# Convolution stem, forward and backward: one leaf product shared by the even and odd halves of the last five chunks of the input gradient

## The chip, the cores and the metric

The kernel runs on one core of a Trainium2 chip. Times are device microseconds of one execution. The kernel before takes 1117.52 us, the median of three runs (1116.88, 1117.52, 1117.68). One more execution was recorded by the profiler; its rows are what the profile shows.

A core has a matrix engine (TensorE, PE in the profile, its weight loads PEld), which writes its sums to PSUM; VectorE (DVE) and ScalarE (ACT) for element-wise work; GpSimd (POOL) and SyncE (SP), which here mostly issue transfers. Each engine takes its instructions in the order in which they were written into its queue.

## The reference

A strided convolution over time, a normalisation over time for each channel, and a GELU; and the gradients of all that.

```python
def _fwd_reference(x, w, gn_gamma, gn_beta):          # x (2, 16000, 256), w (31, 256, 256)
    s = 2
    L = (T - K) // s + 1                              # 7985
    h = jnp.einsum('blc,cd->bld', x[:, 0:s * L:s, :], w[0])
    for i in range(1, K):
        h = h + jnp.einsum('blc,cd->bld', x[:, i:i + s * L:s, :], w[i])
    mu = jnp.einsum('bld->bd', h)[:, None, :] / L
    var = jnp.einsum('bld->bd', (h - mu) ** 2)[:, None, :] / L
    h = (h - mu) / jnp.sqrt(var + 1e-5)
    h = h * gn_gamma[None, None, :] + gn_beta[None, None, :]
    return _gelu(h)
...
    _out, _vjp = jax.vjp(_f, x, w, gn_gamma, gn_beta)
    _grads = _vjp(grad_out)
    _out0 = jnp.asarray(_out)
    return (_out0, *[jnp.asarray(_g) for _g in _grads])
```

Everything is bf16. `out_1` is the gradient of `x`: each of its rows is a sum over taps of the gradient of the convolution's output times a transposed weight.

## The kernel before

**Products.** The 31 taps are split by three binary digits. Two of them are treated as in Karatsuba's multiplication of polynomials: instead of four products of halves there are three (of the first halves, of the last halves, and of sums or differences). Done twice, this gives three branches A, B, C (the order of work is B, A, C, `ORDER`), and in each of them three leaf products, again A, B and C. Sums and differences of inputs and of weights are made on DVE beforehand; the leaf products are corrected and added up afterwards.

**Stages.** F0 and F1 are the forward pass of the two batches (matmul line L505), G0 and G1 the gradient of the input (`input_grad`, matmul line L1131), W the gradient of the weight (matmul line L1346). The gradient of the input goes over two batches `b`, four chunks `c` of 256 positions (one position is 16 rows of `out_1`), two halves `pr` of 128 positions in each, and the three branches. With t = 4b + c, the chunks t = 3 to 7 are the last five; in them all three branches take the shorter way with a shared outer product (the set `GOC`), which before only branch B does.

**One branch of one half, in the last five chunks.** Two PSUM pairs, `px` and `pt`, each hold two banks of 512 columns. The stationary operand of a matmul is 128 positions of the (summed) gradient, the moving one 512 columns of weights.
- `g_outer(pt, ..., C_)`: 4 matmuls; ACT copies the result into `px` (`g_copy`, L1160).
- `g_three_b`: the middle leaf's first part, 4 matmuls on top of that copy; ACT copies bank 0 of `px` to bank 1 (L1160).
- `g_outer(pt, ..., A)`: 4 matmuls; `g_delta` copies the result to SBUF (L1160, out to the arena).
- `g_three_ac(px, br, B_, ...)`: the middle leaf's second part, two groups of 4 matmuls, one for each bank.
- `g_seed`: DVE writes `pt` as `px` less the saved copy (L1194), as the start for leaf A.
- `last(A)` and `last(C_)`, called while the next branch is under way: two groups of 4 matmuls each, then `g_evac`.

`g_evac` moves finished banks out of PSUM: for branch B to `GSB`, for A and C by ACT (`keep`, L584) into the output tile `HO`, to which DVE adds `GSB` (L1208). Each half has an output tile of its own (`HO[pr]`); after branch C's last leaf one transfer of 1 MB writes the 128 positions to `out_1`, issued by SP (the helper `load`, L313). Sums for the next chunk are made by DVE in `g_sums` (L1077) and `e_comp` (L1028), in the same stretch of time. Leaf operands for W are turned by DMA (L318) and stored to DRAM (`dl_turn`).

**Order.** A planner (`Plan`) records each operation, 3333 in all, with what it reads and writes; the order in which they are emitted, and so the order within each engine's queue, is a table of operation numbers in the kernel's text (`SEQUENCE`). Nothing is scheduled at run time: an instruction waits for its inputs by semaphores, and what stands behind it on its engine waits with it.

**Seam to W.** W begins with `leaf_d` (L1512: four subtractions of 2304 elements, into the tiles `DL`), `pair_x` (L1412, L1416) and `pair_d` (L1427, L1432), all on DVE; `DL` lies at byte 146880 of the arena, and `HO[1]` at 144128 reaches over it. SP's queue is shared by the stores of `out_1`, the loads of `x` and the turns.

Of the kernel before, what the change touches and what calls it, by code (L numbers as in the profile page):

```python
# [234 lines left out]
def conv_stem_kernel(  # L235
# [123 lines left out]
    DNO = {True: [sb(GREG + 28928 + 2048 * i, 2, 2, D) for i in range(4)], False: [sb(GREG + o, 2, 2, D) for o in (0, 2048, 25088, 27136)]}  # L359
    assert GREG + 37952 <= REG  # L360

    DG, DGT = sb(209664, P), sb(209920, P)
    ident = DGT


# [767 lines left out]

    def g_wide(br, lf, q):
        return 512 if i_tap(3 - q, 1, MIR[br], MIR[lf]) < K else 256

    def g_leaf(ps, br, lf, pl, o, fresh):
        w2 = W2[MIR[br]]
        for e in range(2):
# [546 lines left out]
```

## Time and profile before

| | us |
|---|---|
| median of three runs | 1117.52 |
| profiled execution, its own time | 1116.78 |
| its span, from the first to the last instruction | 1115.0 |
| PE busy in the span | 1089.1 |
| DVE busy | 920.6 |
| ACT busy | 577.9 |
| PE at L505 (forward), busy | 396.3 |
| PE at L1131 (gradient of the input), busy | 390.3 |
| PE at L1346 (gradient of the weight), busy | 302.8 |

Matmuls overlap, so the busy time of PE is the time in which at least one of them is under way, and the mean duration of one is longer than the distance between two starts. A group of instructions in the profile is named by line, engine, operation and operands (out, then in); behind a bar stand its busy time, the mean duration in ns, and the idle time just before its instructions with what ended most of it. L1131 and L505 and the like are lines of the kernel before. The chain of waits goes back from the last instruction to what released each one.

### The profile page before, as it was taken

To read this page: it belongs to the slowest core of one execution; us is meant where nothing else is said; L and a number is where in the kernel's file an instruction comes from. 1 tells how busy PE (TensorE), PEld (TensorE's weight loads), DVE (VectorE), ACT (ScalarE), POOL (GpSimd) and SP (SyncE) were. 2 spreads that over 40 slices of the span, in tenths; PEclk is the share of its full clock that TensorE was granted. 3 is DMA by queue.
4 is the path that set the end of the run, shared out by engine and by line. 5 is a ranking of instruction groups with operands and counts; after the bars stand their busy time and mean duration, and the time that the engine had idled before them with its cause. 6 is when DMAs were issued, how large, how long until landed. Compare 5 with 4: busy or idle time off the path is not lost.

```text
span 1115.0 us, 18978 instructions
## 1 busy us (share of the span) xinstructions
PE 1089.1 (98%) x7672; PEld 749.7 (67%) x7672; DVE 920.6 (83%) x894; ACT 577.9 (52%) x880; POOL 130.1 (12%) x233
## 2 busy tenths in 40 slices
PE   6999999999999989999999999999999999999997
PEld 4888899978787974444444444444586777678884
DVE  6986877889999999989897565554799699799995
ACT  1234434588988679899964666554413322202221
POOL 0000000000000003232342423231200000000000
PEclk9999999999999999999999999999999999999999
DMA  9969889867979789999899787778985867998778
GB/s 236 189 181 241 249 222 256 223 149 173 224 168 207 252 317 273 266 248 263 215 236 238 173 195 180 177 209 183 279 277 165 257 201 240 287 269 288 229 209 195
DMA packets 343398, 251.96 MB, mean 226 GB/s; under 512 B 234039, under 2 KB 311485, under 8 KB 338109
## 3 DMA queue, kind: packets, MB, share of 16 engines
q1 hardware_dynamic: 336205, 231.86, 80.5%
q0 software_dynamic: 7104, 18.89, 6.2%
q8 instruction: 60, 0.98, 0.3%
q14 instruction: 29, 0.24, 0.1%
HBM read 112.53 MB, written 82.35 MB: 175 GB/s over the span
## 4 chain that ended last, share of the span: by engine, by line
PE 84%; DVE 7%; SPq 2%; DMA 2%; issue 2%; ACT 1%; POOL 1%; DVEq 0%; POOLq 0%
PE ps L505 32%; PE ps L1131 30%; PE ps L1346 22%; SPq L313 1%; DVE arena L447 1%; DVE arena L463 1%; SPq L318 1%; DVE arena L580 1%; DVE arena L1311 1%; DMA out_dram<-arena 1%; DMA arena<-hd 1%; DVE ps L1456 1%; DMA arena<-in_w_dram 1%; DMA arena<-arena 0%; DVE arena L1416 0%
## 5 line engine op out<-in xcount | busy, mean ns | idle before, releaser
L505 PE MATMUL ps<-arena 128*128 128x256 bf16 (+4 forms) x3464 | 396.3, 278 | 10.5 <-DMA arena<-in_x_dram 6.0
L1131 PE MATMUL ps<-arena 128*128 128x512 bf16 (+1 forms) x1824 | 390.3, 376 | 4.3 <-ACT ps L1160 4.0
L505 PEld LDWEIGHTS <-arena 128*128 128x128 bf16 x3464 | 338.0, 98 | 68.5 <-DMA arena<-in_x_dram 6.2
L1131 PEld LDWEIGHTS <-arena 128*128 128x128 bf16 x1824 | 178.6, 98 | 215.6 <-issue 3.6
L1346 PE MATMUL ps<-arena 128*128 128x256 bf16 (+1 forms) x2384 | 302.8, 290 | 5.3 <-DVE arena L580 1.9
L1346 PEld LDWEIGHTS <-arena 128*128 128x128 bf16 x2384 | 233.1, 98 | 75.1 <-issue 6.4
L584 ACT ACTIVATE arena<-ps 128x1024 bf16<-128x1024 f32 (+1 forms) x121 | 122.3, 1022 | 233.0 <-PE ps L1346 79.1
L463 DVE TENSOR_TENSOR arena<-arena 128x2064 bf16<-128x2064 bf16 (+8 forms) x131 | 163.3, 1264 | 28.6 <-PE ps L505 27.7
L313 POOL DMA_DIRECT2D dld<-arena x144 | 105.6, 735 | 239.0 <-DMA arena<-arena 195.1
L1194 DVE TENSOR_TENSOR ps<-ps,arena 128x1024 f32<-128x1024 f32 x36 | 44.3, 1231 | 69.3 <-PE ps L1131 65.4
L1077 DVE TENSOR_TENSOR arena<-arena 128x1032 bf16<-128x1032 bf16 (+1 forms) x114 | 89.3, 813 | 2.7 <-PE ps L1131 1.7
L550 ACT ACTIVATE ps<-ps 128x256 f32<-128x256 f32 x89 | 36.6, 412 | 87.9 <-PE ps L505 81.8
L1311 DVE TENSOR_TENSOR arena<-arena 128x4096 bf16<-128x4096 bf16 x32 | 72.3, 2283 | 1.9 <-DMA arena<-in_x_dram 1.8
L1160 ACT COPY ps<-ps 128x512 f32<-128x512 f32 x84 | 48.2, 575 | 34.0 <-PE ps L1131 32.6
L322 POOL MEMSET arena<- 128x104 bf16 (+11 forms) x52 | 12.3, 253 | 414.9 <-DVE arena L880 138.1
L918 DVE TENSOR_TENSOR arena<-arena 128x2048 bf16<-128x2048 bf16 (+1 forms) x48 | 57.4, 1197 | 3.0 <-ACT arena L921 1.3
L604 ACT ACTIVATE arena<-ps 128x512 bf16<-128x512 f32 (+1 forms) x64 | 37.0, 585 | 32.4 <-PE ps L505 31.4
L1432 DVE TENSOR_TENSOR arena<-arena 128x2048 bf16<-128x2048 bf16 x40 | 47.8, 1216 | 3.1 <-DMA arena<-dld 1.7
L880 DVE TENSOR_TENSOR arena<-arena 128x2048 bf16<-128x2048 bf16 (+1 forms) x40 | 47.6, 1197 | 2.0 <-ACT arena L872 0.9
L1456 DVE TENSOR_TENSOR ps<-ps,arena 128x1024 f32<-128x1024 f32 x24 | 29.0, 1224 | 16.7 <-PE ps L1346 12.6
L1448 ACT COPY ps<-ps 128x256 f32<-128x256 f32 x54 | 19.1, 360 | 43.0 <-PE ps L1346 42.0
L1517 DVE TENSOR_TENSOR arena<-arena 128x4608 bf16<-128x4608 bf16 x16 | 40.5, 2549 | 0.0
(91 smaller groups left out, 746.9 us busy)
## 6 DMA issues: line engine op xcount, KB each, us to landing
arena<-in_x_dram SPq DMA_DIRECT2D x36, 1024.0 KB
arena<-hd SPq DMA_DIRECT2D x40, 512.0 KB
dld<-arena POOLq DMA_DIRECT2D x144, 128.0 KB, 4.3
out_dram<-arena SPq DMA_DIRECT2D x14, 1024.0 KB
arena<-dld SPq DMA_DIRECT2D x18, 640.0 KB
arena<-dld SPq DMA_DIRECT2D x18, 576.0 KB
vl<-arena SPq DMA_DIRECT2D x36, 256.0 KB
arena<-vl SPq DMA_DIRECT2D x9, 1024.0 KB
```

The costliest lines, as they stand in the source:

```text
L313: lambda: e.dma_start(out=out, in_=in_), dma=np_ * ns / 16e3 * 1.03, ns=ns, tp=SH[pk], slack=slack)
L463: lambda: nc.vector.tensor_tensor(out=o, in0=a, in1=b, op=ALU.add))
L505: yield nc.tensor.matmul(ps[:, dh, cs], lhsT=wt, rhs=mv, start=s0, stop=False, skip_group_check=True)
L584: lambda: nc.scalar.activation(out=out, in_=ps, func=ACT.Copy, scale=scale))
L880: add("DVE", dve(nf), [o], [a, b_], lambda: V.tensor_tensor(out=o, in0=a, in1=b_, op=op))
L918: add("DVE", dve(nf), [o], [a, b_], lambda: V.tensor_tensor(out=o, in0=a, in1=b_, op=op))
L1077: lambda: nc.vector.tensor_tensor(out=o, in0=a, in1=b, op=ALU.subtract))
L1131: yield nc.tensor.matmul(ps[:, e, 0:wide], lhsT=lt, rhs=mv, start=s0, stop=False, skip_group_check=True)
L1160: add("ACT", act(512), [o], [i], lambda: nc.scalar.copy(out=o, in_=i))
L1311: add("DVE", dve(4096), [o], [a, b], lambda: nc.vector.tensor_tensor(out=o, in0=a, in1=b, op=ALU.add))
L1346: yield nc.tensor.matmul(ps[:, s, c0:c1], lhsT=lt, rhs=mv, start=s0, stop=False, skip_group_check=True)
L1432: add("DVE", dve(2048), [o], [u, v], lambda o=o, u=u, v=v: nc.vector.tensor_tensor(out=o, in0=u, in1=v, op=ALU.subtract))
```

## The change

Only for t = 4b + c of 3 and more:

1. The two halves of a chunk are no longer its first and last 128 positions, but its even and its odd ones. The stationary operand is read with a step of two elements (`win`).
2. In branch B the middle leaf is made in another way. Both halves need one product in common, since an odd position's neighbour is an even one: `x_common` makes it once a chunk (4 matmuls, with the weight sum `WS`) and `keep`s it in SBUF (`HX`). For each half `x_own` makes 4 matmuls and a DVE operation that writes both banks of `px` as bank 1 plus `HX`; `x_rest` then adds two groups of 2 matmuls with the difference `DX` of neighbouring positions (`x_diff`, DVE) as stationary operand. `g_three_b` with its ACT copy and `g_three_ac` fall away there.
3. There is one output tile `HO` instead of two; `WS` and `HX` lie in the space of the second, `DX` behind the other tiles.
4. Each half's store is split in two: the rows of branch A after A's last leaf, the rows of branch C after C's, 0.5 MB each in runs of 1024 bytes, to every second block of 16 rows.
5. One more sum on DVE makes `WS`, once, and the table `SEQUENCE` is another over the whole program, with 3369 operations.

```diff
-    HO = [sb(119232, 2, 4, 512), sb(GREG + 16704, 2, 4, 512)]
+    HO = sb(119232, 2, 4, 512)
...
+    XB = B_
+    WS, HX = sb(GREG + 16704, 2, 2, 512), sb(GREG + 20800, 1024, dt=FP32)
+    DX = sb(209056, 2, 2, P)
...
+    def win(o, k):
+        s0, st_ = o
+        return slice(s0 + k, s0 + k + st_ * (P - 1) + 1, st_)
+
+    def x_diff(u, par):
+
+        def at(k):
+            return u.rearrange("p e d f -> p (e d) f")[:, :, k:k + 2 * P - 1:2]
+        o = DX.rearrange("p e d f -> p (e d) f")
+        add("DVE", dve(o.free_size(), 1), [o], [u], lambda: nc.vector.tensor_tensor(out=o, in0=at(2 * par), in1=at(1), op=ALU.subtract))
+
+    def x_common(px, u):
+        for e in range(2):
+            jobs = [(e, 512, u[:, e, dh, win((1, 2), 0)], WS[:, dh, 1 - e], dh == 0) for dh in range(2)]
+            g_mm(px, jobs, [px[:, e]], [WS, u[:, e]])
+        keep(HX, flat2(px))
+
+    def x_own(px, br, pl, o):
+        wd = W2D[MIR[br], B_]
+        g_mm(px, [(1, 512, pl[1][:, dh, win(o, q2)], wd[:, dh, 1 - q2], False) for q2 in range(2) for dh in range(2)],
+             [px[:, 1]], [wd, pl[1], px[:, 1]])
+        v = px[:, 1]
+        v = bass.AP(tensor=v.tensor, offset=v.offset, ap=[list(v.ap[0]), [0, 2], [1, 512]])
+        h = HX.rearrange("p (e f) -> p e f", e=2)
+        add("DVE", dve(1024, 1), [px[:]], [px[:, 1], HX], lambda: nc.vector.tensor_tensor(out=px[:], in0=v, in1=h, op=ALU.add))
+
+    def x_rest(px, br, par):
+        w2 = W2[MIR[br]][:, B_]
+        for e in range(2):
+            k = 3 - 2 * par - e
+            jobs = [(e, 512, DX[:, e, dh], w2[:, dh, k * 512:k * 512 + 512], False) for dh in range(2)]
+            g_mm(px, jobs, [px[:, e]], [w2, DX[:, e], px[:, e]])
...
-                jobs.append((0, 512, pl[1][:, dh, o + q2:o + q2 + P], wd[:, dh, 1 - q2, :], fresh and q2 + dh == 0))
+                jobs.append((0, 512, pl[1][:, dh, win(o, q2)], wd[:, dh, 1 - q2, :], fresh and q2 + dh == 0))
...
-        if br == C_ and lf == C_:
-            n0 = 512 * c + 256 * pr
...
+        if lf == C_ and 4 * b + c >= 3:
+            m0, r = HM * c + pr, P if c < 3 else 116
+            dst = bass.AP(tensor=out_1.tensor, offset=out_1.offset + (b * T + 16 * m0) * C + 512 * r2,
+                          ap=[[32 * C, r], [1024, 4], [1, 512]])
+            load(dst, ho[0:r].rearrange("p e k f -> p (e k) f")[:, r2:8:2], r * 4096, 1024, "POOL", slack=60.0)
...
-                    o = P * pr
+                    o = (P * pr, 1) if t < 3 else (pr, 2)
...
+                            four = t >= 3 and br == XB
+                            if four:
+                                x_diff(GU[br], pr)
+                                if pr == 0:
+                                    x_common(px, GU[br])
                             g_outer(pt, br, planes(br, C_), o, C_)
-                            g_copy(px[:, 0], pt[:, 0])
-                        g_three_b(px, br, B_, planes(br, B_), o, not both)
+                            g_copy(px[:, int(four)], pt[:, 0])
+                        if both and four:
+                            x_own(px, br, planes(br, B_), o)
+                        else:
+                            g_three_b(px, br, B_, planes(br, B_), o, not both)
...
-                        g_three_ac(px, br, B_, GU[br], o)
+                        if both and four:
+                            x_rest(px, br, pr)
+                        else:
+                            g_three_ac(px, br, B_, GU[br], o)
...
+            w2 = W2[MIR[XB]][:, B_].rearrange("p d (q f) -> p d q f", q=4)
+            w_sum(WS, w2[:, :, 0:2], w2[:, :, 2:4])
```

The same change from `o + q2:o + q2 + P` to `win(o, q2)` stands in `g_leaf`, `g_outer` and `g_three_ac`. In the changed kernel the lines behind this place are some fifty further down: L1077 becomes L1081, L1194 L1230, L1208 L1244, L1311 L1362, L1412 L1463, L1416 L1467, L1427 L1478, L1512 L1563.

**The order, first place.** The last half of the last chunk on DVE before, from the sums of its operands on: L1194 is the seed of leaf A in a branch, L1208 the addition to the output tile, L1077 the sums of operands.

```order
L1077 TENSOR_TENSOR arena<-arena 128x2x2x258
L1208 TENSOR_TENSOR arena<-arena 128x4x512
L1077 TENSOR_TENSOR arena<-arena 128x8x258
L1194 TENSOR_TENSOR ps<-ps,arena 128x1024
L1208 TENSOR_TENSOR arena<-arena 128x4x512
L1077 TENSOR_TENSOR arena<-arena 128x8x258 x2
L1194 TENSOR_TENSOR ps<-ps,arena 128x1024 x3
L1208 TENSOR_TENSOR arena<-arena 128x4x512 x2
```

The same place in the changed kernel: L1150 is `x_diff`, L1165 the DVE operation of `x_own`, L1230 the seed of leaf A, L1244 the addition to the output tile.

```order
L1165 TENSOR_TENSOR ps<-ps,arena 128x1024
L1244 TENSOR_TENSOR arena<-arena 128x4x512
L1230 TENSOR_TENSOR ps<-ps,arena 128x1024
L1150 TENSOR_TENSOR arena<-arena 128x512
L1081 TENSOR_TENSOR arena<-arena 128x2x2x258
L1244 TENSOR_TENSOR arena<-arena 128x4x512
L1081 TENSOR_TENSOR arena<-arena 128x8x258 x2
L1230 TENSOR_TENSOR ps<-ps,arena 128x1024 x2
L1244 TENSOR_TENSOR arena<-arena 128x4x512 x2
L1165 TENSOR_TENSOR ps<-ps,arena 128x1024
L1230 TENSOR_TENSOR ps<-ps,arena 128x1024
```

The operation of `x_own`, for which the matmuls of `x_rest` wait, now stands in the queue behind additions to the output tile, and `x_diff` stands early, behind the seed of the branch before.

**Second place: the seam to W on DVE.** Before, the last addition to the output tile (L1208) comes ahead of half of `pair_d` (L1427), `pair_x` (L1412), the four operations of `leaf_d` (L1512) and two more of `pair_x` (L1416).

```order
L1208 TENSOR_TENSOR arena<-arena 128x4x512
L1427 TENSOR_TENSOR arena<-arena 128x1024 x2
L1208 TENSOR_TENSOR arena<-arena 128x4x512
L1427 TENSOR_TENSOR arena<-arena 128x1024 x2
L1412 TENSOR_TENSOR arena<-arena 128x4096
L1512 TENSOR_TENSOR arena<-arena 128x2304 x4
L1416 TENSOR_TENSOR arena<-arena 128x2048 x2
L1456 TENSOR_TENSOR ps<-ps,arena 128x1024 x2
L1432 TENSOR_TENSOR arena<-arena 128x2048 x2
```

In the changed kernel, with L1478 for L1427, L1563 for L1512, L1244 for L1208, L1463 for L1412, L1467 for L1416, L1483 for L1432 and L1507 for L1456:

```order
L1478 TENSOR_TENSOR arena<-arena 128x1024 x4
L1563 TENSOR_TENSOR arena<-arena 128x2304
L1244 TENSOR_TENSOR arena<-arena 128x4x512 x2
L1563 TENSOR_TENSOR arena<-arena 128x2304 x2
L1463 TENSOR_TENSOR arena<-arena 128x4096
L1467 TENSOR_TENSOR arena<-arena 128x2048 x2
L1563 TENSOR_TENSOR arena<-arena 128x2304
L1483 TENSOR_TENSOR arena<-arena 128x2048
```

All four of L1478 and the first of L1563 have moved ahead of the last two additions, and the last of L1563 behind L1467. `leaf_d` no longer writes where an output tile lay; the first L1483, whose target reaches over `HO`, comes seven operations behind the last addition.

**Third place: the start, on DVE.** Before, in the first chunk of the forward pass: L463 are sums of inputs, L447 differences of weights, L580 leaf results moved out of PSUM.

```order
L447 TENSOR_TENSOR arena<-arena 128x2048 x12
L463 TENSOR_TENSOR arena<-arena 128x16x262
L463 TENSOR_TENSOR arena<-arena 128x8x260
L447 TENSOR_TENSOR arena<-arena 128x2048
L463 TENSOR_TENSOR arena<-arena 128x8x260
L447 TENSOR_TENSOR arena<-arena 128x2048
L463 TENSOR_TENSOR arena<-arena 128x8x258
L463 TENSOR_TENSOR arena<-arena 128x2x4x262 x2
L580 TENSOR_TENSOR arena<-ps,arena 128x1024
L463 TENSOR_TENSOR arena<-arena 128x8x260 x2
L580 TENSOR_TENSOR arena<-ps,arena 128x1024
L447 TENSOR_TENSOR arena<-arena 128x2048 x2
```

The changed kernel there, with L467, L451 and L584 for them; the memset of L1642, which was at L1591 and stood later, now comes in ahead of these rows:

```order
L467 TENSOR_TENSOR arena<-arena 128x8x260 x2
L451 TENSOR_TENSOR arena<-arena 128x2048
L467 TENSOR_TENSOR arena<-arena 128x2x4x262
L467 TENSOR_TENSOR arena<-arena 128x8x258
L451 TENSOR_TENSOR arena<-arena 128x2048
L467 TENSOR_TENSOR arena<-arena 128x2x4x262
L584 TENSOR_TENSOR arena<-ps,arena 128x1024
L467 TENSOR_TENSOR arena<-arena 128x8x260
L584 TENSOR_TENSOR arena<-ps,arena 128x1024
L451 TENSOR_TENSOR arena<-arena 128x2048
L467 TENSOR_TENSOR arena<-arena 128x8x260
L451 TENSOR_TENSOR arena<-arena 128x2048
```

One L467 has moved behind the L451 that follows the second L584.

More of the change, by code (lines that the diff above doesn't have):

```diff
@@ L359, in conv_stem_kernel @@
     DNO = {True: [sb(GREG + 28928 + 2048 * i, 2, 2, D) for i in range(4)], False: [sb(GREG + o, 2, 2, D) for o in (0, 2048, 25088, 27136)]}
+    XB = B_
+    WS, HX = sb(GREG + 16704, 2, 2, 512), sb(GREG + 20800, 1024, dt=FP32)
+    DX = sb(209056, 2, 2, P)
     assert GREG + 37952 <= REG
[L362 removed]
+    DG, DGT = sb(210080, P), sb(210336, P)
     ident = DGT
@@ L1143, in g_leaf @@
                 u = pl[(e + q) % 2]
-                oo = o + (e + q) // 2
                 for dh in range(2):
-                    jobs.append((e, wide, u[:, dh, oo:oo + P],
+                    jobs.append((e, wide, u[:, dh, win(o, (e + q) // 2)],
                                  w2[:, MIR[lf], dh, (3 - q) * 512:(3 - q) * 512 + wide], fresh and q + dh == 0))
@@ L1164, in g_outer @@
         wd = (W2DO if lf == A else W2DC)[MIR[br]]
-        jobs = [(0, 512, pl[1][:, dh, o + q2:o + q2 + P], wd[:, dh, 1 - q2, :], lf == C_ and q2 + dh == 0)
+        jobs = [(0, 512, pl[1][:, dh, win(o, q2)], wd[:, dh, 1 - q2, :], lf == C_ and q2 + dh == 0)
                 for q2 in range(2) for dh in range(2)]
@@ L1176, in g_three_ac @@
                 for dh in range(2):
-                    jobs.append((e, wide, u[:, e, dh, o + q2:o + q2 + P],
+                    jobs.append((e, wide, u[:, e, dh, win(o, q2)],
                                  w2[:, MIR[lf], dh, (3 - q) * 512:(3 - q) * 512 + wide], False))
@@ L1200, in g_evac @@
         both = (b, c, br) in GOC
-        ho = HO[pr if both else 0]
+        ho = HO
         r2 = 0 if br == A else 1
@@ L1212, in g_evac @@
                 lambda: nc.vector.tensor_tensor(out=ho[:, :, k, :], in0=ps[:], in1=g, op=ALU.add))
-        if br == C_ and lf == C_:
-            n0 = 512 * c + 256 * pr
-            r = P if c < 3 or pr == 0 else 104
-            load(out_1[b, 8 * n0:8 * n0 + 16 * r, :].rearrange("(p r) c -> p (r c)", r=16),
-                 ho[0:r].rearrange("p e k f -> p (e k f)"), r * 8192, 4096, "POOL", slack=60.0)
+        if lf == C_ and 4 * b + c >= 3:
[3 more added lines that the diff above has]
+            load(dst, ho[0:r].rearrange("p e k f -> p (e k) f")[:, r2:8:2], r * 4096, 1024, "POOL", slack=60.0)
+        elif br == C_ and lf == C_:
+            m0 = HM * c + P * pr
+            load(out_1[b, 16 * m0:16 * (m0 + P), :].rearrange("(p r) c -> p (r c)", r=16),
+                 ho.rearrange("p e k f -> p (e k f)"), P * 8192, 4096, "POOL", slack=60.0)
     G3 = {(b, br, B_) for b in range(NB) for br in ORDER}
```

205 rows, old and new, of the table SEQUENCE are left out of this document.

## The prediction

> **What bounds the kernel now.** I read the page first: the busy shares, the chain that ended last, the costliest groups.
>
> ```profile
> PE 1089.1 (98%) x7672; PEld 749.7 (67%) x7672; DVE 920.6 (83%) x894; ACT 577.9 (52%) x880; POOL 130.1 (12%) x233
> PE ps L505 32%; PE ps L1131 30%; PE ps L1346 22%; SPq L313 1%; DVE arena L447 1%; DVE arena L463 1%; SPq L318 1%; DVE arena L580 1%; DVE arena L1311 1%; DMA out_dram<-arena 1%; DMA arena<-hd 1%; DVE ps L1456 1%; DMA arena<-in_w_dram 1%; DMA arena<-arena 0%; DVE arena L1416 0%
> ```
>
> TensorE is busy for 98% of the span, and its three matmul lines (forward L505, input gradient L1131, weight gradient L1346) carry the chain. The 98% is a mean over stages, so the table of windows comes next, cut where PE's idle stretches begin and end. Its columns are the busy time of PE, PEld, DVE, ACT and POOL, each with its count, then the granted clock, the DMA share and GB/s.
>
> ```profile
> 406.00:570.00 164.00, 159.70 (x753) 73.46 (x751) 152.30 (x179) 147.47 (x184) 48.89 (x83) 1.00 1.03 252
> 570.00:801.00 231.00, 231.00 (x1081) 105.75 (x1080) 139.15 (x162) 127.86 (x166) 70.00 (x118) 1.00 0.84 204
> 801.00:817.00 16.00, 14.94 (x134) 12.82 (x132) 13.30 (x13) 5.22 (x9) 0.18 (x1) 1.00 0.95 306
> 1020.00:1076.00 56.00, 51.75 (x467) 45.48 (x466) 56.00 (x43) 8.45 (x12) 0.00 (x0) 1.00 0.79 265
> ```
>
> The last five chunks of the input gradient are the stretch from 570 to 801: PE has no gap at all at a granted clock of 1.00, while DVE is busy for 139.15/231 = 60% and ACT for 55%. There the number of matmuls alone sets the time. Behind it, from 801 to 817, stands the seam to the weight gradient, where PE does wait. The groups of PE in that stretch, kept apart by shape (busy, mean ns of one, idle before):
>
> ```profile
> L1131 PE MATMUL ps<-arena 128*128 128x512 bf16 x1057 | 230.0, 379 | 0.0
> L1131 PE MATMUL ps<-arena 128*128 128x256 bf16 x20 | 3.8, 273 | 0.0
> L1131 PEld LDWEIGHTS <-arena 128*128 128x128 bf16 x1076 | 105.4, 98 | 124.8 <-issue 0.2
> ```
>
> A matmul lasts 379 ns from start to end, but they overlap: 230.0 us over 1057 of 512 columns and 20 of half that width, 1067 in all, is **0.2156 us from start to start**. A weight load takes 98 ns beside it, and the loading side idles for 124.8 us.
>
> **The change part by part.** *Matmuls removed.* The middle leaf of branch B takes 4 + 8 matmuls in each half now, 24 in a chunk. Afterwards it takes 4 once a chunk (`x_common`) and 4 + 4 in each half, 20. Five chunks: 20 × 0.2156 = **−4.31 us**, all of it in the gapless stretch, if that stays gapless.
>
> *Strided weight loads.* In the five chunks 1020 weight loads now read every second position. No row of before shows that. From below it costs nothing. From above, what counts is the pitch: a load is hidden until it takes 216 ns, 2.2 times the 98 of its row. The nearest row is that same load with a stride of one; I take 0. [...]
>
> *What the shared part puts between matmuls.* Rows of the chunks' DVE and ACT groups:
>
> ```profile
> L1194 DVE TENSOR_TENSOR ps<-ps,arena 128x1024 f32<-128x1024 f32 x30 | 37.0, 1232 | 68.5 <-PE ps L1131 64.7 <-ACT arena L1160 3.8
> L1077 DVE TENSOR_TENSOR arena<-arena 128x1032 bf16<-128x1032 bf16 x49 | 32.3, 689 | 0.5 <-POOL arena L322 0.5
> L1028 DVE TENSOR_TENSOR arena<-arena 128x512 bf16<-128x512 bf16 x8 | 3.4, 421 | 0.0
> L584 ACT ACTIVATE arena<-ps 128x1024 bf16<-128x1024 f32 x59 | 59.3, 1023 | 61.0 <-PE ps L1131 57.4 <-DVE arena L1208 3.4
> L1160 ACT COPY ps<-ps 128x512 f32<-128x512 f32 x59 | 33.9, 576 | 28.6 <-PE ps L1131 27.4 <-DVE arena L1212 0.4
> ```
>
> DVE gets ten adds in PSUM (the form of L1194, 1.232 each) and ten `x_diff` of 512 elements (between 0.421 and 0.689; I take 0.5): 10 × 1.73 = 17.3 us on an engine that idles for 92 us there. ACT loses ten copies of 0.576 and gets five `keep`s of 1.023: 0.6 us less. So neither becomes the bound on average; what counts is how many matmuls lie between a producer and its consumer. A matmul's end lies 0.379 − 0.216 = 0.16 behind the start of the next, and the chain of waits at the seam shows 0.02 from PE's end to ACT, 0.02 from ACT to DVE, 0.05 from DVE to PE:
>
> ```profile
> 801.23 0.02 issue
> 801.25 1.03 ACT arena L584
> 802.29 0.02 issue
> 802.31 1.24 DVE arena L1208
> 803.55 0.02 issue
> 803.56 0.34 SPq L313
> ...
> 803.96 7.61 DMA out_dram<-arena
> 811.57 0.04 issue
> 811.62 2.62 DVE arena L1512 x2
> 814.24 0.32 DVE arena L1416
> 814.55 0.73 issue
> 815.29 1.23 DVE arena L1416
> 816.52 0.05 issue
> 816.57 13.49 PE ps L1346 x122
> ```
>
> From `x_own` over the add to `x_rest`: 0.16 + 0.02 + 1.23 + 0.05 = 1.46 us, and the order of PE has at least 8 matmuls between them, 1.73 us: hidden, with 0.27 to spare. From `x_common` over `keep` and copy to `x_own`: 0.16 + 0.02 + 1.02 + 0.02 + 0.58 + 0.05 = 1.85 against 8 matmuls, 1.73, at the tightest place: 0.12 of waiting. A copy alone takes 0.16 + 0.02 + 0.58 + 0.05 = 0.81, and some have just 4 matmuls, 0.86. The DVE is in order, so an add that meets an element-wise operation ahead of it (0.69 of L1077) is up to 0.4 late. I take three such places at 0.1: **+0.3**; between 0 and 10 × 0.4 = 4.
>
> *The seam.* DVE's `leaf_d` (L1512) there waited for a store, since the second half's buffer lay under it. The timeline (start, busy, engine, line, wait before):
>
> ```profile
> 810.34 3.90 DVE L1512 TENSOR_TENSOR arena<-arena 128x2304 bf16<-128x2304 bf16 x3 [2.13 <-DMA out_dram<-arena]
> 811.76 0.42 PEld L1346 LDWEIGHTS <-arena 128*128 128x128 bf16 x4 [0.23 <-issue]
> 813.02 3.22 PE L1346 MATMUL ps<-arena 128*128 128x256 bf16 x28 [0.67 <-DVE arena L1512]
> 816.57 1.70 PE L1346 MATMUL ps<-arena 128*128 128x256 bf16 x14 [0.33 <-DVE arena L1416]
> 804.66 2.28 DVE L1412 TENSOR_TENSOR arena<-arena 128x4096 bf16<-128x4096 bf16 x1
> ```
>
> PE's window there shows 16.00 − 14.94 = 1.06 us idle, in three gaps (0.06 at 811.75, 0.67, 0.33); each costs 0.16 more, since without it the next matmul would have begun before the last one's end: 0.22 + 0.83 + 0.49 = 1.5 us. The second output buffer is gone, so `leaf_d` waits for no store. In its place `pair_d` does, further back. DVE's row after the last evacuation add (ending at 803.55 in this trace's time) becomes 2 × 1.31 + 2.28 + 2 × 1.23 + 1.31 = 8.7 us, to 812.2; PE asks for the result of L1512 there at 812.2 and for that of L1416 at 816. So both waits about vanish, the 0.2 of ACT stays: **−1.2** of 1.5. The last store, half the bytes of one of the two that together took 7.61, has these 8.7 us before `pair_d` reads over it; were it late, the wait comes back: 0 at worst.
>
> *The start and the rest of the table.* The order was made anew everywhere. At the start PE waits for DVE's row:
>
> ```profile
> 45.64 2.35 DVE L447 TENSOR_TENSOR arena<-arena 128x2048 bf16<-128x2048 bf16 x2
> 46.91 1.27 PE L505 MATMUL ps<-arena 128*128 128x256 bf16 x10 [0.56 <-DVE arena L447]
> L463 DVE TENSOR_TENSOR arena<-arena 128x2080 bf16<-128x2080 bf16 x5 | 6.1, 1239 | 0.0
> L1591 DVE MEMSET arena<- x1: 485/485/485, 76.1 to 76.1; 128x512 uint32 x1
> ```
>
> Ahead of that point one L463 of 1.24 goes away, the memset of 0.49 comes in, and the matmul there now needs the operation behind the L447, again 1.24: +0.5 at most, −0.75 if the old one still decides. I take **+0.4**. Between 406 and 570 (4.3 us idle) and 1020 and 1076 (4.25) the same operations stand in a slightly other order; one DVE operation to either side is ±1.2, taken as 0.
>
> *Stores.* Ten of 1 MB become twenty of 0.5 MB in runs of 1024 bytes, on SP's in-order queue, where one costs 0.34 to issue. At a DMA share of 0.84 there is room, and no PE wait in the chunks is a DMA's: taken as 0, priced under the rivals.
>
> Sum: −4.31 + 0.3 − 1.2 + 0.4 = −4.8. The profiled execution took 1116.78 us (span 1115.0 and 1.78 around it), 0.74 below the median of 1117.52; so 1112.0 against it and **1112.7 against the median**.
>
> **Rivals.** (1) *The gain is eaten inside the chunks*: the new adds and copies stall PE. For it: margins of 0.05 and 0.27 us, on a DVE in order. Against it: before has its L1194 adds with 7 to 8 matmuls around them, and PE has no wait in the stretch. At 0.3 in each of ten halves, and the seam as before: −4.31 + 3 + 0.4, about 1116.6: no change.
> (2) *Slower, by one buffer for two.* ACT's evacuation of a half must now wait until the store of the half before has left the same buffer, and that store stands in SP's queue behind other waits:
>
> ```profile
> SPq L313 <- DVE arena L1028: 24.2, 5, 8.1
> SPq L318 <- DMA dld<-arena: 35.2, 9, 6.7
> ```
>
> At the tightest place some 34 matmuls, 7.3 us, lie between the store's place in the order and the next write; a store held up as these rows show (up to 8.1, or by transfers of 6.7) comes too late, and ACT, whose next copy PE needs within 0.86, hands it on. It turns the sign from 0.5 us a half (4.8/10); at 1 us a half the time is 1112.7 + 10 = 1122.7. Against it: most places have more than 8.5 us, and a store of a quarter of the 7.61's bytes should land within half of that.
> (3) *The strided loads show.* From 216 ns on, each ns costs 1.02 us; sign turned at 221 ns; at 2.5 times 98, 245 ns, +30: 1142. Only an unknown read penalty speaks for it.
> (4) *All stalls vanish*, start and re-ordering helping: −4.31 − 1.5 − 0.8 = −6.6: 1110.9.
>
> **How the numbers follow.** Chances: forecast 0.60, rival 1 0.16, rival 2 0.11, rival 3 0.05, rival 4 0.08. What a measurement of this kernel can tell from no change is about 0.2%, 2.2 us, so faster means below 1115.3. Faster: 0.60 + 0.08 + a fifth of the cases of rivals 1 and 2 (stalls of half the size), 0.06: 0.74. Within 0.2%: most of rival 1 and the mild end of 2, 0.15. Slower: the rest of 2, and 3, 0.11. The range leaves out rival 3 and the heavy end of 2: from 1110.7 (rival 4) to 1116.8 (rival 1 in full).
>
> **What would show it.** In the profile after, 7652 matmuls; in the five chunks PE without gaps and some 4.3 us shorter, with loads still near 98 ns and under 216; a wait of PE for `x_own`'s add, for its copy or for an evacuation, each in tenths, would be the stalls of rivals 1 and 2, and ACT waiting for a DMA to out_dram would be rival 2's sign. At the seam no wait of `leaf_d` for a store, and PE's first matmuls without the 0.67. At 47 us PE's wait for DVE should be within a microsecond of 0.56. The forecast is wrong if the stretch still takes 231 us, or if the gain comes from another stage than these two.

## The result, and the profile after

The changed kernel takes **1165.3 us**, the median of five runs (1164.61 to 1168.95), against 1117.52 for the kernel before in five (1116.52 to 1117.68): a ratio of 1.0437 [1.0422, 1.0451], 4.4% slower. The profiled execution has a span of 1162.8 us. The loss stands in the stretch that was to gain. The page of the changed kernel, busy shares and the chain by engine and by line:

```profile
PE 1097.6 (94%) x7603; PEld 751.9 (65%) x7652; DVE 940.5 (81%) x915; ACT 576.9 (50%) x875; POOL 129.2 (11%) x233
PE 75%; DVE 10%; DMA 7%; SPq 3%; ACT 3%; issue 3%; DVEq 0%; ACTq 0%
PE ps L509 34%; PE ps L1135 20%; PE ps L1397 20%; DMA out_dram<-arena 6%; SPq L319 2%; DVE arena L922 2%; ACT arena L588 1%; DVE arena L1081 1%; DVE ps L1507 1%; DVE arena L1248 1%; DVE arena L1362 1%; DVE arena L1483 1%; DMA arena<-arena 1%; SPq L314 1%; DVE arena L584 1%
```

There are 7652 weight loads, 20 fewer than before, as the edit says. Stores to DRAM (`out_dram<-arena`) take 6% of the span in the chain, where they took 1% before. The table of windows (columns as in the prediction) shows the place; first the kernel before from 570 us to the end of its seam, then the changed kernel from 570 to the end of its own, whole and with two pieces of it.

```profile
570.00:817.00 247.00, 245.94 (x1213) 118.56 (x1212) 152.45 (x174) 133.08 (x175) 70.18 (x118) 1.00 0.85 210
```

```profile
570.00:870.00 300.00, 259.62 (x1220) 124.48 (x1240) 177.69 (x201) 135.54 (x175) 73.12 (x123) 0.94 0.77 175
...
620.00:670.00 50.00, 36.89 (x141) 15.48 (x143) 24.98 (x33) 14.66 (x21) 12.30 (x18) 0.83 0.69 129
...
720.00:770.00 50.00, 47.23 (x218) 21.71 (x222) 30.87 (x35) 30.85 (x39) 17.73 (x40) 1.00 0.77 187
```

PE idles for 300.00 − 259.62 = 40.4 us there, where it idled for 1.06. A second loss stands beside it: the mean granted clock is 0.94. The longer stretch holds 1240 weight loads to 1212; with 20 matmuls of 0.2156 us gone and 48 of W come in (W's pace in the prediction's last window is 51.75/467 = 0.11 us), PE would be busy for 245.94 − 4.3 + 5.3 = 246.9, and it is 259.6: some 13 us of matmuls that ran slower. Idle, 39.3 more than before, and clock together make 52 of the 53 us between forecast and result. Who waits: first the largest of ACT's waits before, from 560 to 812, then ACT's in the changed kernel from 560 to 870, then PE's there (total us, times, longest).

```profile
ACT arena L584 <- PE ps L1131: 58.1, 37, 5.3
```

```profile
ACT arena L588 <- PE ps L1135: 54.9, 29, 12.3
ACT arena L588 <- DMA out_dram<-arena: 37.1, 6, 10.5
```

```profile
PE ps L1135 <- ACT ps L1196: 13.5, 2, 8.5
PE ps L1135 <- ACT arena L588: 12.4, 4, 5.7
PE ps L1397 <- DVE arena L1483: 6.8, 1, 6.8
PE ps L1135 <- DVE ps L1165: 6.2, 1, 6.2
```

The list of before has no row for a DMA at all. The second of ACT's rows after the change is the one that the prediction named as the sign of its rival 2: ACT, at an evacuation, waits for a transfer to `out_1`. The chain of waits (start, us, what) shows how that reaches PE:

```profile
597.55 10.32 DMA out_dram<-arena
607.87 0.02 issue
607.91 0.04 issue
607.96 1.03 ACT arena L588
608.99 0.02 issue
609.01 0.58 ACT ps L1196
609.59 0.04 issue
609.63 6.37 PE ps L1135 x20
...
619.24 8.88 DMA out_dram<-arena
...
853.63 10.21 DMA out_dram<-arena
```

A store takes 10.32 us; the evacuation (L588) starts 0.09 behind it, ACT's copy (L1196) behind that, and PE, which needs the copy, behind both. The store at 853.63 is the last one: `pair_d` (L1483) writes over the output tile and waits for it, which is PE's wait of 6.8 at the seam.

What is wrong with these stores is seen in the DMA view: 40 equal slices of a short window, each digit the busy share of the 16 DMA engines in tenths. First a store of 116 positions, then one of 128, both of the changed kernel:

```profile
DMA  7342322222222222235458999592232299191111
DMA packets 1014, 0.67 MB, mean 92 GB/s; under 512 B 533, under 2 KB 996, under 8 KB 1014
```

```profile
DMA  1599899999998989999999899999999999986310
DMA packets 528, 0.52 MB, mean 308 GB/s; under 512 B 16, under 2 KB 528, under 8 KB 528
```

The first window is 7.3 us long (640.1 to 647.4), and for its first half a quarter of the engines work, 2 to 3 tenths; the second is 1.7 us long (700.4 to 702.1), and nearly all of them do, 8 to 9 tenths. By the trace's packets a store of 116 moves its 464 runs of 1024 bytes with three to four under way at a time, in 7.1 to 8.8 us; the one of 128 moves 512 runs with some fourteen under way, in 1.65 us. The last chunk of each batch has 232 positions: before they were stored as 128 and 104, by even and odd ones they are 116 and 116. Two halves, two branches, two batches: eight such stores.

### The profile page after: what moved, and what is told of

It is laid out like the page before. It is cut to its first block, busy times and chain, and to the rows that moved or that the text cites. A ratio compares the mean times of both kernels' runs of the same rounds, so it can differ in the third digit from the quotient of the medians.

```text
span 1162.8 us, 18943 instructions
## 1 busy us (share of the span) xinstructions
PE 1097.6 (94%) x7603; PEld 751.9 (65%) x7652; DVE 940.5 (81%) x915; ACT 576.9 (50%) x875; POOL 129.2 (11%) x233
## 4 chain that ended last, share of the span: by engine, by line
PE 75%; DVE 10%; DMA 7%; SPq 3%; ACT 3%; issue 3%; DVEq 0%; ACTq 0%
PE ps L509 34%; PE ps L1135 20%; PE ps L1397 20%; DMA out_dram<-arena 6%; SPq L319 2%; DVE arena L922 2%; ACT arena L588 1%; DVE arena L1081 1%; DVE ps L1507 1%; DVE arena L1248 1%; DVE arena L1362 1%; DVE arena L1483 1%; DMA arena<-arena 1%; SPq L314 1%; DVE arena L584 1%
## 5 line engine op out<-in xcount | busy, mean ns | idle before, releaser
L1135 PE MATMUL ps<-arena 128*128 128x512 bf16 (+1 forms) x1767 | 396.4, 384 | 38.8 <-ACT ps L1196 17.4
L1397 PE MATMUL ps<-arena 128*128 128x256 bf16 (+1 forms) x2372 | 305.1, 291 | 11.5 <-DVE arena L1483 7.1
L1397 PEld LDWEIGHTS <-arena 128*128 128x128 bf16 x2384 | 234.3, 98 | 82.4 <-issue 12.2
L588 ACT ACTIVATE arena<-ps 128x1024 bf16<-128x1024 f32 (+1 forms) x126 | 127.5, 1022 | 285.4 <-PE ps L1397 102.2
L467 DVE TENSOR_TENSOR arena<-arena 128x2064 bf16<-128x2064 bf16 (+8 forms) x131 | 163.3, 1266 | 28.2 <-PE ps L509 27.3
L1081 DVE TENSOR_TENSOR arena<-arena 128x1032 bf16<-128x1032 bf16 (+1 forms) x114 | 90.2, 814 | 7.0 <-PE ps L1135 4.7
L1230 DVE TENSOR_TENSOR ps<-ps,arena 128x1024 f32<-128x1024 f32 x36 | 44.3, 1232 | 54.8 <-PE ps L1135 44.8
L1362 DVE TENSOR_TENSOR arena<-arena 128x4096 bf16<-128x4096 bf16 x32 | 72.8, 2286 | 6.1 <-DMA arena<-xsd 2.3
L1483 DVE TENSOR_TENSOR arena<-arena 128x2048 bf16<-128x2048 bf16 x40 | 48.4, 1222 | 15.3 <-PE ps L1397 8.4
L1244 DVE TENSOR_TENSOR arena<-arena 128x2048 bf16<-128x2048 bf16 x20 | 24.5, 1223 | 41.2 <-ACT arena L588 30.8
L1196 ACT COPY ps<-ps 128x512 f32<-128x512 f32 x74 | 42.6, 576 | 24.6 <-PE ps L1135 22.8
```

The costliest lines, as they stand in the source:

```text
L467: lambda: nc.vector.tensor_tensor(out=o, in0=a, in1=b, op=ALU.add))
L588: lambda: nc.scalar.activation(out=out, in_=ps, func=ACT.Copy, scale=scale))
L1081: lambda: nc.vector.tensor_tensor(out=o, in0=a, in1=b, op=ALU.subtract))
L1135: yield nc.tensor.matmul(ps[:, e, 0:wide], lhsT=lt, rhs=mv, start=s0, stop=False, skip_group_check=True)
L1230: lambda: nc.vector.tensor_tensor(out=pt[:], in0=px[:], in1=i, op=ALU.subtract))
L1362: add("DVE", dve(4096), [o], [a, b], lambda: nc.vector.tensor_tensor(out=o, in0=a, in1=b, op=ALU.add))
```

## The experiments

Three theories, by the names of the expectations. **FEW ENGINES**: a store of 116 positions is spread over too few DMA engines, and what waits for its tile waits too long. **FALSE OVERLAP** (formed only from the chain of the store issued by ACT, below): rows of A and of C lie in `HO` by turns, so an evacuation of one branch waits for the store of the other, though they share no byte. **QUEUE**: such a store also holds up what is issued behind it. Rivals were the strided weight loads, the matmuls as the bound and the place of the store in the order. Line numbers behind the edit shift by a few: L1397 is L1405 in these kernels, and in those with blocks it is L1407, and L1244 is L1246.

**The store of 116 as 112 + 4, and as 58 + 58.** The helper's transfer becomes two.

```diff
-            load(dst, ho[0:r].rearrange("p e k f -> p (e k) f")[:, r2:8:2], r * 4096, 1024, "POOL", slack=60.0)
+            src = ho[0:r].rearrange("p e k f -> p (e k) f")[:, r2:8:2]
+            def parts():
+                a = 0
+                for n in (112, 4) if r == 116 else (r,):          # e2_58_58: (58, 58)
+                    d = bass.AP(tensor=dst.tensor, offset=dst.offset + 32 * C * a, ap=[[32 * C, n], [1024, 4], [1, 512]])
+                    yield nc.sync.dma_start(out=d, in_=src[a:a + n])
+                    a += n
+            add("SP", 0.5, [dst], [src], parts, dma=1.0, slack=60.0)
```

> The eight stores of 116 positions are issued as 112 and 4 positions each; nothing else is changed. In the changed kernel their 464 packets of 1024 bytes come at 53 to 65 a microsecond, about 4 at a time, and need 7.3 to 8.8 us from the first to the last, while the stores of 128 positions, of the same packets, come at up to 311 a microsecond, 16 at a time. Theory FEW ENGINES (a store is spread over as many of the 16 DMA engines as divide its number of positions: 116 gives 4, 112 gives 16): the packets of the 112 pass at 200 a microsecond or more, each store lands within about 3 us, ACT's waits for a store fall from 37.1 us to under 10, and the time falls by 35 to 48 us, to 1117 to 1130; what stays above 1112.7 is late issue. Theory SHORT RUNS (runs of 1024 bytes at a step of 16 KB are slow in themselves): the rate stays near 60 a microsecond, the time within 5 us of 1165. Theory LATE ISSUE (the stores are issued too late in SP's queue; the landing matters little): the time falls by less than 10 us.

> The same eight stores as 58 and 58 positions. FEW ENGINES: 58 is divided by 2 alone, so each part runs on 2 engines; if both use the same two, the store needs about twice as long as now (464 packets at some 30 a microsecond, 15 us), and the time rises by 30 to 60 us, to 1195 to 1225; if they use different ones, it stays near 1165. SHORT RUNS and LATE ISSUE: no change, 1165 within 5.

Measured: 112 + 4 takes 1131.07 us, 1.0129 [1.0112, 1.0146]; 58 + 58 takes 1200.75, 1.0752 [1.073, 1.0773]. One cut takes 34 us off, the other puts 35 on, with the same bytes and the same number of transfers. The chain with 58 + 58:

```profile
597.24 14.20 DMA out_dram<-arena
...
623.92 12.24 DMA out_dram<-arena
```

14.20 us for the store that took 10.32 whole. By the trace's packets the two parts of 58 need 13.4 us with 1.8 runs under way on average, 112 + 4 need 2.07 us with 12.6. FEW ENGINES holds for the sizes run here, and it is a matter of the number 116 and not of its bytes; SHORT RUNS is out, since the runs of 1024 bytes are the same. Runs under way on average are 3 to 3.7 for 116 whole, 1.8 for 58 + 58, 12.6 for 112 + 4 and 14.4 for 128; how the number of engines follows from other sizes was not shown. But with 112 + 4 ACT still waits for the store:

```profile
ACT arena L588 <- DMA out_dram<-arena: 28.4, 7, 8.8
```

Under 10 us of waiting and 1117 to 1130 us of time were expected: both missed, the time by 1 us. Something else makes ACT wait.

**Loads with a step of one; the common product twice.** Both on top of 112 + 4.

```diff
-        return slice(s0 + k, s0 + k + st_ * (P - 1) + 1, st_)                  # e3_step1
+        return slice(s0 + k, s0 + k + P)
...
-            ... WS[:, dh, 1 - e], dh == 0) for dh in range(2)]                  # e4_common2
+            ... WS[:, dh, 1 - e], i + dh == 0) for i in range(2) for dh in range(2)]
```

> As the kernel with 112 and 4, but every stationary operand is read with a step of one element instead of two (the positions are then not the even and odd ones, so the gradient of x is another). If the strided weight loads cost nothing, the time is that of the kernel with 112 and 4 within 1.5 us and the loads stay at 98 to 99 ns; if they cost 5 ns each beyond cover, it is 5 us less.

> As the kernel with 112 and 4, but the common product issues each of its matmuls twice: 4 more a chunk, 20 in all, as many as the change saves (the common product is then doubled, so the gradient of x is another). If a matmul in these chunks is worth its 0.2156 us, the time is 4.3 us more (3.5 to 5); if the chunks are bound by stores or by DVE and ACT, 0 to 2 us more.

Measured: a step of one takes 1130.95 us, 1.0133 [1.0118, 1.0148], the same as 1131.07. The group of the weight loads from 570 to 800 reads, without the step:

```profile
L1135 PEld LDWEIGHTS <-arena 128*128 128x128 bf16 x978 | 96.9, 99 | 133.2 <-issue 23.2 <-DVE arena L1081 0.3
```

and with it, in the kernel of 112 + 4:

```profile
L1135 PEld LDWEIGHTS <-arena 128*128 128x128 bf16 x977 | 96.6, 99 | 133.4 <-issue 23.0 <-DVE arena L1081 0.3
```

99 ns both times, in 978 and 977 loads: the step of two elements cost nothing here; larger steps were not run. Twenty more matmuls gave 1131.92, 1.0142 [1.012, 1.0164], 0.85 us more where the prediction's pace makes 4.31. The two intervals, of some 2 us to either side, overlap, so the 0.85 itself is not clear of noise; it fits a stretch in which, as long as the waits are there, matmuls more or fewer are mostly hidden in them.

**The store earlier, and from another queue.** In the first kernel each half-store stands right behind its addition in `SEQUENCE`; in the second ACT issues it, some 10 matmuls behind the addition.

```diff
-                    yield nc.sync.dma_start(out=d, in_=src[a:a + n])            # e6_act
+                    yield nc.scalar.dma_start(out=d, in_=src[a:a + n])
```

> As the kernel with 112 and 4 (1131.1 us), but in the order each of the twenty half stores stands right behind the addition that finishes its rows, instead of up to 60 matmuls behind it; no other operation is moved. That kernel's profile shows ACT waiting 28.4 us for stores to leave the output tile, in 7 waits up to 8.8, and two stores landing 8.1 and 8.3 us after their issue, behind two loads of 0.5 MB that SP issued just ahead of them. Theory ONE TILE (what is left of the loss is the single output tile, whose store comes late in SP's queue and lands behind what was issued before it): the waits fall to some 10 us, the time to 1117 to 1125. Theory ORDER (what is left comes from the remade order of start, seam and weight gradient): 1129 to 1133.

> As the kernel with 112 and 4, but the twenty half stores are issued by ACT instead of SP, each placed ten matmuls behind the addition that finishes its rows. They then stand behind no turn and no load in SP's queue; ACT spends some 0.4 us on each of 28 transfers, on an engine that is busy for 55% there. ONE TILE: stores land within 3 to 4 us, hardly any wait of ACT for a store is left, and the time is 1111 to 1117. ORDER: 1129 to 1135.

Measured: 1148.55 us, 1.0286 [1.0266, 1.0307], and 1137.69, 1.0182 [1.0164, 1.02]. Both missed; both are slower than 112 + 4 alone. SP takes its instructions in order, so a store moved ahead waits there for its addition and what stands behind it waits along: in the first kernel SP waits 57.6 us at stores for additions (19 times), in 112 + 4 alone 31.7 us (10 times), in the changed kernel 36.5 us (12 times, from 560 to 870). That the same happens on ACT's queue in the second is likely, not shown. ACT still waits 26.5 and 27.3 us for stores. The chain of the second kernel told why:

```profile
593.35 1.03 ACT arena L588
594.38 0.02 issue
594.40 1.24 DVE arena L1244
595.64 0.02 issue
595.66 4.88 DMA out_dram<-arena
600.54 0.02 issue
600.56 1.03 ACT arena L588
```

The addition to A's rows ends at 595.64, the store of A's rows follows at once, and the evacuation at 600.56 waits for it, 4.9 us after the addition. That is C's evacuation, into C's rows, which this store does not read. The built program says the same of the changed kernel: at C's second evacuation of the first half the wait for a DMA is part of the instruction (DMAHW3_49 is the semaphore that the store of A's rows raises). With the rows in blocks, below, it is not.

```
after:             L588 ACTIVATE arena<-ps 128x2x512 [waits DMAHW3_49,PE_49]
rows in blocks:    L588 ACTIVATE arena<-ps 128x2x512 [waits PE_49]
```

It holds the other way round too. In the changed kernel the store of A's rows stands in the order behind C's first evacuation, and it waits for that evacuation besides the addition that finishes its own rows; C's second evacuation then waits for the store. In its chain, for the second half of that chunk:

```profile
637.81 1.03 ACT arena L588
...
638.86 8.98 DMA out_dram<-arena
...
647.92 1.03 ACT arena L588
```

**Nobody waits for the store.** On top of 112 + 4 the store reads a weight tile, so that no wait for `HO` is left; the second kernel also makes the common product twice, the third leaves the 116 whole.

```diff
-            src = ho[0:r].rearrange("p e k f -> p (e k) f")[:, r2:8:2]
+            src = sb(49152, 2, 4, 512)[0:r].rearrange("p e k f -> p (e k) f")[:, r2:8:2]
...
-                for n in (112, 4) if r == 116 else (r,):                        # e8_other116
+                for n in (116,) if r == 116 else (r,):
```

> As the kernel with 112 and 4, but the half stores read a weight tile that is not written before the weight gradient, instead of the output tile (so the gradient of x is another): same transfers at the same places, but nothing waits for them to leave the output tile. ONE TILE: no wait of ACT for a store, PE without gaps in the five chunks, and the time falls by about 20 us (the gaps of PE in the chunks and the slower clock behind them), to 1110 to 1114, which is the forecast without the store. ORDER: 1127 to 1133.

> As the kernel whose stores read a weight tile, with each matmul of the common product issued twice, 20 more in all (gradient of x another). If the five chunks are then without gaps, these cost what the 20 saved ones were to bring: 4.3 us more than without them (3.5 to 5). If something else than matmuls sets the chunks' time, under 2 us.

> As the kernel whose half stores read a weight tile (1112.2 us, gradient of x another), but the eight stores of 116 positions are one transfer each, on 4 engines. Nothing waits for these stores to leave the output tile, so what is left is what they do to other transfers. Theory TILE ONLY: the stores on 4 engines cost through the output tile alone; the time is 1111 to 1114. Theory QUEUE: each engine works its queue off in order, so the loads and turns issued behind such a store wait for their share on those 4 engines (in the kernel with blocks and 116 whole, a load of 0.5 MB issued behind one took 8.9 us and DVE waited for it): the time is 1118 to 1135.

Measured: 1112.24 us, 0.996 [0.9944, 0.9975]; 1116.87, 1.0001 [0.9992, 1.001]; 1129.76, 1.0121 [1.0108, 1.0134]. The first is the forecast's kernel, without the store's waits. (Here a store doesn't wait for its addition either, so SP's queue runs a little freer than the change could have it; the kernel with blocks, where it does wait, comes within 1.4 us below.) The second is 4.63 above it, at 20 matmuls: now the stretch is bound by matmuls, and the term of −4.31 is right within the intervals, which leave 2.6 to 6.6. The third is QUEUE alone: with no one waiting for the tile, eight stores of 116 whole still cost 17.5 us, and PE idles for 15.4 us from 570 to 850 in place of 0.85. SP's queue behind a store in the first of the five chunks shows how, first in that third kernel, then in the first:

```profile
613.59 16.14 SPq L319 DMA_TRANSPOSE arena<-arena  x7
...
630.40 0.43 SPq L314 DMA_DIRECT2D arena<-dyd  x1
```

```profile
611.12 10.06 SPq L319 DMA_TRANSPOSE arena<-arena  x7
...
622.37 0.44 SPq L314 DMA_DIRECT2D arena<-dyd  x1
```

Seven turns behind the store hold SP for 16.14 us in place of 10.06; the first of them, right behind it, alone takes 5.35 in place of 2.16. The load of the next operands (`dyd`), which stands behind the turns in the same queue, is issued 8.0 us later. In what order an engine takes its own transfers, of which the theory speaks, no view shows; the run shows the delay.

**Rows of A and of C in blocks of their own.** On top of 112 + 4; the second kernel leaves the 116 whole.

```diff
-            keep(ho[:, :, k, :], ps[:])
+            own = 4 * b + c >= 3
+            hs = sb(119232, 2, 2, 2, 512)[:, r2] if own else ho[:, :, r2:r2 + 3:2, :]
+            keep(hs[:, :, 0 if lf == A else 1, :], ps[:])
             if lf == C_:
-                v, g = ho[:, :, r2:r2 + 3:2, :], ...
+                v, g = hs, ...
...
-            src = ho[0:r].rearrange("p e k f -> p (e k) f")[:, r2:8:2]
+            src = hs[0:r].rearrange("p e l f -> p (e l) f")
```

> As the kernel with 112 and 4, but in the last five chunks the output tile holds branch A's rows as one block of 4 KB a partition and branch C's as another, instead of rows of A and C by turns; the same bytes go to the same place. In the changed kernel's trace the first evacuation into C's rows of a half waits for the store of A's rows of the same half, issued just before, though they share no byte, and A's evacuations in the next half wait for C's store: the semaphores see the two sets of rows, which lie between each other, as one. Theory FALSE OVERLAP: with the blocks apart each evacuation waits for its own rows' store alone, issued a half before; at least 34 matmuls, 7.3 us, lie between; the waits of ACT for stores fall from 28.4 us to under 6, PE has no gap over 1 us in the chunks, and the time is 1111 to 1116. Theory LATE STORE (the single tile is too little even so, the stores being issued late and landing in up to 8 us): 1122 to 1131.

> As the kernel with the rows of A and C in blocks of their own, but the eight stores of 116 positions are one transfer each again, as in the changed kernel. It tells how much each cause costs alone: if the eight stores on 4 engines (7 to 9 us from issue to landing) matter only through the false overlap, the time is within 4 us of the kernel with blocks and 112 and 4 (1112 to 1118); if they also outlast the real distance, waits remain in the two chunks with 116 positions and at the seam, and the time is 1118 to 1140.

Measured: **1113.67 us**, 0.9967 [0.9956, 0.9978], and 1139.41, 1.0202 [1.0185, 1.022]. In the first, the largest of ACT's waits from 560 to 850, and the windows:

```profile
ACT arena L588 <- PE ps L1135: 58.9, 40, 4.5
```

```profile
570.00:800.00 230.00, 228.69 (x1052) 105.02 (x1072) 158.09 (x184) 129.83 (x165) 67.05 (x117) 1.00 0.85 204
```

No wait of ACT for a store is left in that list, PE idles for 1.3 us in 230, and the clock is 1.00. Same data, same order of the operations, and the store is no faster: its 464 runs take 2.07 us by the trace's packets in both kernels. FALSE OVERLAP holds. The four kernels make a table (us):

| | 116 whole | 112 + 4 |
|---|---|---|
| rows by turns | 1165.3 | 1131.07 |
| rows in blocks | 1139.41 | 1113.67 |

Either cause alone is enough to make the kernel slower than before: 14 us for the overlap, 22 for the few engines, 48 for both. The 22 are not the queue alone: with blocks and 116 whole, ACT still waits 12.9 us for stores, in two waits.

**The order of before for the start.** On top of blocks and 112 + 4, the first 1460 operations of `SEQUENCE` stand in the order of before.

> As the kernel with the rows in blocks and 112 and 4 (1113.7 us), with the order of the first 1460 operations (forward pass and the beginning of the gradient of the input) as in the kernel before; they are the same operations. Against the kernel before, the traces show 0.9 us more waiting of PE up to 47 us, 0.3 up to 406 and 1.0 from there to 570. If the remade order is the cause, the time falls by 1 to 2 us, to 1111.5 to 1112.7; if not, it stays within 0.7 of 1113.7.

Measured: **1111.1 us**, 0.9955 [0.9943, 0.9967], the fastest of all, and 0.45% faster than the kernel before. It is 2.6 us below 1113.67, somewhat more than was expected of the order, but that the order is the cause is not shown: the two intervals overlap, and the traces speak against it. One copy of ACT in the first of the five chunks begins at 589.26 us in this trace, and with the new order at 589.25 in the changed kernel and in 112 + 4, at 589.87 in the kernel whose store no one waits for and at 592.15 in the one with blocks. Executions with the same order lie as far apart as the gain that was looked for.

## Why the prediction was wrong

The step that failed is *Stores*: "At a DMA share of 0.84 there is room, and no PE wait in the chunks is a DMA's: taken as 0". Both halves of the sentence are true of the kernel before, where a half's store had a tile of its own and nothing waited for it soon. With one tile the store became a producer, and its time had to be priced by its shape and by who waits for it. The term taken as 0 measured 53 us: 1165.3 against 1112.24 with stores of 112 + 4 for which no one waits, 17.5 of them through the queue alone.

- **Rival 2 was the mechanism, with the wrong size and a chance of 0.11.** It priced a wait of 1 us a half, 1122.7; ACT waits for stores 37.1 us. Two things were missing. "A store of a quarter of the 7.61's bytes should land within half of that" came from two stores of 128 and 104 positions; those of 116 take 8.55 to 10.32 on the chain, and no row of before has a store of 116. And "some 34 matmuls, 7.3 us" was counted to the next write of the same rows. The write that waits is that of the other branch. With rows in blocks, where neither waits for a store, C's two evacuations begin 2.5 and 4.6 us behind the end of the addition to A's rows (at 599.33 and 601.43; the addition ends at 596.8). In the changed kernel the store has to fit between the end of the first and the start of the second, 1.1 us, and even a store of 112 + 4 needs 3.28 at this place on the chain of its kernel.
- **Matmuls, −4.31: right.** 4.63 for 20 matmuls, where nothing else holds the stretch (1112.24 against 1116.87, each within about 1 to 2 us).
- **Strided loads, 0: right**, 99 ns with and without the step.
- **Stalls in the chunks, +0.3; seam, −1.2; start, +0.4; the rest, 0.** In the kernel whose store no one waits for, the windows are:

```profile
406.00:570.00 164.00, 159.21 (x755) 73.70 (x754) 152.96 (x179) 145.06 (x180) 46.56 (x81) 1.00 1.08 257
570.00:796.00 226.00, 225.21 (x1053) 102.90 (x1051) 153.63 (x181) 127.82 (x163) 65.75 (x115) 1.00 0.85 203
796.00:812.00 16.00, 15.93 (x126) 12.13 (x125) 15.86 (x14) 6.91 (x12) 4.33 (x6) 1.00 1.07 318
```

  PE idles for 0.8 us in the chunks, more than the 0.3 of the forecast, for 0.07 at the seam in place of 1.06, and for 4.8 from 406 to 570 in place of 4.3. Up to 47 us it idles for 11.45 in place of 10.48, a loss of 1.0 and not of 0.4; waits for loads of `x` (7.3 in place of 6.0) and not for DVE make it. One `x_diff` takes 0.68, not 0.5. The seam came as worked out, given that store; with the store as it is, the step's "0 at worst" was wrong too: `pair_d` waits for it, and PE 6.8 us for `pair_d`.
- **What the sum lacked at the end.** PE's last piece in the chain, and the last operation of DVE behind it, are 2.06 us earlier there than before:

```profile
1094.79 12.40 PE ps L1405 x89
1107.19 0.02 issue
1107.21 0.42 DVE arena L1434
```

  (before: the same operation at 1109.27), while the span is 1110.8 against 1115.0, 4.2 shorter. So 2.1 us of the gain lies behind the last matmul, in the last stores of W, where the prediction had nothing (in the trace of every kernel with the change 3.1 to 3.2 us lie behind the end of that operation, before 5.3); ahead of it the work was 4.3 shorter, and stalls and order gave back about 2.2 (the forecast: a gain of 0.5 from them). That 1112.24 falls so near to the forecast of 1112.7 is thus in part two errors that cancel.
- Rivals 1, 3 and 4 are not what happened; rival 1's copies and additions do wait, but behind the store. The bounds of the range, 1110.7 and 1116.8, are 0.2 wider than the sums of rivals 4 and 1, 1110.9 and 1116.6; that changes nothing here.

## What to carry to other kernels

When a buffer is dropped, price the transfer that empties it as a producer: its shape first (here 116 positions, the size of the tail chunk alone, had 3 to 3.7 runs under way, where 112 + 4 had 12.6 and 128 had 14.4), then every later write that the semaphores take for an overlap, which need not share a byte with it. A transfer off the critical path has no price in the profile of before, and "there is room" on the DMA engines on average says nothing of one with three to four runs under way. A size of 116 is mended by 112 + 4, and interleaved rows by blocks; each is an edit of a few lines, worth 34 and 17 us here, and one without the other still lost.

## What the runs showed of the hardware

After a wait of 8.54 us PE did not come back at full speed. The windows of the changed kernel around it:

```profile
601.00:609.60 8.60, 0.09 (x1) 0.00 (x0) 0.59 (x1) 1.59 (x2) 2.19 (x4) 0.63 0.96 94
609.60:614.00 4.40, 4.37 (x12) 1.64 (x12) 1.25 (x2) 1.33 (x2) 2.32 (x4) 0.56 0.98 329
614.00:616.00 2.00, 2.00 (x11) 0.89 (x9) 0.00 (x0) 0.85 (x2) 0.78 (x2) 1.00 0.55 162
```

PE is busy for all of the 4.4 us behind the wait, with 12 matmuls in place of 20, at a granted clock of 0.56; then the clock is 1.00. In shorter windows of the same trace the granted clock is 1.00 from 601 to 603 us, 0.55 from 603 to 605, 0.50 in each of four windows from 605 to 613, and 0.77 from 613 to 614. Taken as one step down and one up between 1.00 and 0.50, the rows with 0.55 and 0.77 give an estimate of when: down at 603.2 (605 − 2.00 × 0.45 / 0.5), some 2.1 us after PE's last matmul, and up at 613.5 (613 + 1.00 × 0.23 / 0.5), 3.8 us after the next one began at 609.63. So the wait of 8.54 us cost 8.54 + 4.37 − 12 × 0.2156 = 10.3. The prediction's prices for its rivals, each wait at its own length, left that out.
